# Attention logits from queries and keys in two rounded fp32 parts, two heads in the two halves of TensorE's rows

## The chip, the cores and the metric

The kernel runs on one core of one Trainium2 chip. The metric is the device time of one execution in microseconds (us). The times before are 1162.42, 1163.57 and 1163.80 us, median 1163.57. The profile is one execution of its own, of 1163.27 us.

## The reference

One input x (2048 rows of 640) goes through a gated mix of two branches.

```python
g = sigmoid((x * gate_w).sum(-1))
# A: 32 heads of 20, four segments of 512 rows, causal softmax inside a segment
logits = einsum("bhqd,bhkd->bhqk", qs, ks) * 20 ** -0.5 + mask
a_dot = softmax(logits) @ vs
a_mem = (phi(qs) @ M) / (phi(qs) @ z + 1e-6)     # M, z: sums over the segments before
o = sigmoid(beta) * a_mem + (1 - sigmoid(beta)) * a_dot
a = o @ wo
# B: SwiGLU with an inner size of 1728
b = (silu(x @ w1) * (x @ w3)) @ w2
out = g * a + (1 - g) * b
```

All inputs and outputs are fp32.

## The kernel before

**Dense work.** Weights and activations are split in two parts that TensorE takes at one pass each (`split`: a rounded fp32 copy by ScalarE, the rest by GpSimd or VectorE), and a product is three matmuls (`PASSES`: high x high, high x low, low x high). `proj` runs 15 matmuls of 128 x 512 for a block of 128 features and 512 rows of x; it serves the projections q and k and the gates g and u of the SwiGLU. Down projection (f), values (v) and output projection (op) run matmuls of 320 columns.

**Logits.** A block of q or k (128 features, 512 rows) leaves PSUM in three bf16 parts (`parts`). Six products of parts are kept. The parts are stored to DRAM as six copies for each feature (`qd`, `kd`, one triple, one pair and one single store), so that a head's 20 features are 120 rows. `load_pair` brings two heads' rows into `qst` and `kst` (four buffers each, in turn), by two DMAs on SyncE's queue. For each head there are two rounds of logits:

- `s_unit`: queries as weights, keys streaming, 120 rows, for the four query blocks of 128, of 128, 256, 384 and 512 columns (causal). VectorE takes the row maxima.
- `max_parts` and `max_rows`: the maxima in three bf16 parts are turned and sent by ScalarE's DMA queue into rows 120 to 122 of `qst`; the same rows of `kst` are -1.
- `st_unit`: keys as weights, queries streaming, 123 rows, so that the maximum is subtracted by the matmul; 512, 384, and 128 with 256 columns. ScalarE takes the exponential into P, GpSimd masks the diagonal blocks.

`pv_quad` multiplies P with the values for four heads at once, each in 32 columns of the array (o, 32 matmuls in plain fp32, two passes for each of the 16 calls).

**Order.** The order of TensorE's instructions is written out by the program; the other engines' order is made by a scheduler, except where `here` (keep in program order) pins it. `attention()` is a generator of small steps, ten to a head: t of the third head before, s of this head in three units, now and then an o block. The main loop takes one step of it and then as much dense work as the pacing gives (`credit`, from the dense work of the segment over its slots). `tick()` counts down delayed actions (`after(n, ...)`), `stores()` delayed stores, `w_step()` loads and splits the coming weights. Before attention starts there is a head of projections for the first two segments, and behind it a tail of down and output projection.

Of the kernel before, what the change touches and what calls it, by code (L numbers as in the profile page):

```python
# [27 lines left out]
KR = 6 * DH  # L28
LAG_T, LAG_P, NP, AGE = 3, 4, 4, 4
# [7 lines left out]
def gated_mix(ctx: ExitStack, tc: tile.TileContext, xT, wqk, wv, w13, w2, w2h, wo, beta, out):  # L37
# [7 lines left out]
    qd = [dp.tile([D, 6, L], BF, name=f"qd{c}") for c in range(NSEG)]  # L45
    kd = [dp.tile([D, 6, L], BF, name=f"kd{c}") for c in range(NSEG)]
# [7 lines left out]
    qst = [cp.tile([P, 2, L], BF, name=f"qst{i}") for i in range(NST)]  # L54
    kst = [cp.tile([P, 2, L], BF, name=f"kst{i}") for i in range(NST)]
# [6 lines left out]
    nsT = [cp.tile([P, 32], BF, name=f"ns{i}") for i in range(2)]  # L62
# [4 lines left out]
    def constants():  # L67
        make_identity(nc, ident)
        nc.gpsimd.memset(mask, 0.0)
        nc.gpsimd.affine_select(mask[:, 384:], mask[:, 384:], pattern=[[-1, P]], base=0,  # L70
                                channel_multiplier=1, compare_op=ALU.is_ge, fill=BIG)
        for i in range(2):
            nc.gpsimd.memset(nsT[i], 0.0)
        for i in range(NST):
            nc.gpsimd.memset(qst[i][96:], 0.0)
            nc.gpsimd.memset(kst[i][96:], -1.0)
# [79 lines left out]
    def w_step():  # L156
# [3 lines left out]
        for r in raws:  # L160
            if clock["step"] - r[3] == (AGE // 2 if "exp" in last else AGE + 2) and r[0] >= 7:
                r[4] = last.get("exp", last["act"])
        if raws and raws[0][0] in EARLY:
            if clock["step"] >= 6 + 2 * raws[0][0]:
                w_split()
        elif raws and raws[0][0] < clock["oldest"] + NW and \
                clock["step"] - raws[0][3] >= (AGE if "exp" in last or raws[0][0] < 7 else AGE + 3):
            w_split()
# [88 lines left out]
    def parts(name, ps, phi=None):  # L257


        s = ht_tile([P, 3, L], BF, name)  # L260
        nc.scalar.copy(s[:, 0], ps)
        if phi is not None:
            e = f_tile("phi_t")
            nc.vector.tensor_scalar(e, ps, 0.0, None, op0=ALU.min)
            nc.scalar.activation(e, e, AF.Exp)
# [4 lines left out]
        last["act"] = nc.scalar.copy(s[:, 1], t)  # L270
        nc.gpsimd.tensor_sub(s[:, 2], t, s[:, 1])
        return s

    def q_block(c, mb, i, alloc, oldest=None):
# [6 lines left out]
        dst = qd[c][mb * P:(mb + 1) * P]  # L281
        store_later(dst[:, 0:3], s[:, 0:1].broadcast_to([P, 3, L]), queue=nc.scalar)
        store_later(dst[:, 3:5], s[:, 1:2].broadcast_to([P, 2, L]), queue=nc.scalar)
        store_later(dst[:, 5], s[:, 2], ("q", c, mb))
# [66 lines left out]
    def k_block(c, mb, i, prev):  # L351
# [12 lines left out]
        dst = kd[c][mb * P:(mb + 1) * P]  # L364
        store_later(dst[:, 0:3], s)
        store_later(dst[:, 3:5], s[:, 0:2])
        store_later(dst[:, 5], s[:, 0], ("k", c, mb))
# [14 lines left out]
    def memory_write(c, mb):  # L382
# [12 lines left out]
        nc.scalar.copy(mt, pm[:, :nh * VE].rearrange("p (h e) -> p h e", e=VE))  # L395
# [104 lines left out]
    oall, heads = {}, {}  # L500

    def load_pair(j):

        c, h = divmod(j, H)
        q, k = qst[j // 2 % NST], kst[j // 2 % NST]
# [15 lines left out]
        for i in range(2):  # L521
            o = VE * (h % 8 + i)
            heads[j + i] = dict(c=c, h=h + i, q=q[:, i], k=k[:, i], pair=q, v=bank["v"][:, :, o:o + 32], m=m)

    def s_unit(j, t):
        u = heads[j]
        q, k, m = u["q"], u["k"], u["m"]
        qbs = ((0, 1), (2,), (3,))[t]
        ps = pp.tile([P, L], F32, tag="s", name=f"s{j}_{t}", bufs=2)
        for qb in qbs:  # L530
            n = P * (qb + 1)
            o = P * qb if qb < 2 else 0
            nc.tensor.matmul(ps[:, o:o + n], q[:KR, qb * P:(qb + 1) * P], k[:KR, :n],  # L533
                             start=qb != 1, stop=qb != 0, skip_group_check=True)
        for qb in qbs:
            n = P * (qb + 1)
            o = P * qb if qb < 2 else 0
            junk = sp.tile([P, L], BF, tag="junk", name="junk", bufs=1)
            a = 4 * (u["h"] % 2) + qb
            nc.vector.tensor_tensor_reduce(out=junk[:, :n], in0=ps[:, o:o + n], in1=mask[:, L - n:],  # L540
                                           scale=1.0, scalar=-3.0e38, op0=ALU.add, op1=ALU.max,
                                           accum_out=m[:, a:a + 1])

    def max_parts(j):

        m = heads[j]["m"]
        r = sp.tile([P, 8], F32, tag="nm", name="nm")
        nt = nsT[j // 2 % 2]
        ns = nt[:, :24].rearrange("p (a b) -> p a b", a=3)
        nc.vector.tensor_copy(ns[:, 0], m)  # L550
        nc.vector.tensor_sub(r, m, ns[:, 0])
        nc.vector.tensor_copy(ns[:, 1], r)
        nc.vector.tensor_sub(ns[:, 2], r, ns[:, 1])
        heads[j]["ns"] = nt

    def max_rows(j):
        mr = sp.tile([32, P], BF, tag="mr", name="mr")
        for g in range(4):
            nc.vector.transpose(mr[:, 32 * g:32 * g + 32], heads[j]["ns"][32 * g:32 * g + 32])
        dst = heads[j]["pair"][KR:KR + 3].rearrange("a h (b n) -> a (h b) n", n=P)  # L560
        after(4, lambda: here(nc.scalar.dma_start(dst, mr[:24])))

    def st_unit(j, t):
        u = heads[j]
        q, k = u["q"], u["k"]
        if t == 0:
            u["P32"] = sp.tile([P, 1280], F32, tag="P32", name=f"P{j}", bufs=NP)
        P32 = u["P32"]
        o, n = ((0, 512), (512, 384), (896, 384))[t]
        ps = pp.tile([P, L], F32, tag="t", name=f"t{j}_{t}", bufs=2)  # L570
        if t < 2:
            nc.tensor.matmul(ps[:, :n], k[:KR + 3, t * P:(t + 1) * P], q[:KR + 3, t * P:], start=True, stop=True)  # L572
            src = ps[:, :n]
        else:
            nc.tensor.matmul(ps[:, :P], k[:KR + 3, 384:], q[:KR + 3, 384:], start=True, stop=False,
                             skip_group_check=True)
            nc.tensor.matmul(ps[:, P:384], k[:KR + 3, 256:384], q[:KR + 3, 256:], start=False, stop=True,  # L577
                             skip_group_check=True)
            src = ps[:, :384]
        last["exp"] = nc.scalar.activation(P32[:, o:o + n], src, AF.Exp, scale=SCALE)  # L580
        if t < 2:
            return
        d0 = P32[:, :1024].rearrange("p (a b) -> p a b", a=2)[:, :, :P]
        d1 = P32[:, 896:1152].rearrange("p (a b) -> p a b", a=2)
        for d in (d0, d1):
            nc.gpsimd.affine_select(d, d, pattern=[[0, 2], [1, P]], base=0, channel_multiplier=-1,  # L586
                                    compare_op=ALU.is_ge, fill=0.0)
# [31 lines left out]
    def o_load(c, b):  # L619
# [3 lines left out]
        f = P * b  # L623
        queue = nc.gpsimd if (c, b) != (NSEG - 1, KB - 1) else nc.sync
        while f < P * (b + 1):
            h, e = divmod(f, DH)
            n = min(DH - e, P * (b + 1) - f) if e else max((P * (b + 1) - f) // DH * DH, min(DH, P * (b + 1) - f))
            dst = oall[c][f - P * b:f - P * b + n, b]
# [4 lines left out]
            f += n  # L633
# [51 lines left out]

    def attention():

        for t in range(-3, NJ + LAG_P):
            js, jt, jp = t, t - LAG_T, t - LAG_P
            order = (("-", 0), ("t", 2), ("s", 0), ("m", 0), ("t", 0), ("s", 1), ("p", 0), ("t", 1), ("s", 2))  # L690
            for kind, i in order:
                if kind == "p" and 0 <= jp < NJ and jp % 4 == 3:
                    pv_quad(jp - 3)
                elif kind == "t":
                    h = jt - 1 if i == 2 else jt
                    if 0 <= h < NJ:
                        st_unit(h, i)
                    if i == 2 and t % 2 and t + 3 < NJ:
                        load_pair(t + 3)
                elif kind == "s" and 0 <= js < NJ:  # L700
                    s_unit(js, i)
                    if i == 2 and js % 2:
                        max_parts(js)
                        max_rows(js)
                tick()
                yield t
            tick()
            yield t
# [123 lines left out]
    segs.append((H + LAG_P + 1, seg))  # L832
# [17 lines left out]
    segs.append((2 * H + LAG_P, seg))  # L850
# [4 lines left out]
    segs.append((3 * H + LAG_P + 1, seg))  # L855
# [5 lines left out]
    segs.append((NJ + LAG_P, seg))  # L861
# [4 lines left out]
    for n, (_, g) in enumerate(head):  # L866
# [3 lines left out]
        if n == 0:  # L870
            constants()
        elif n == 9:
            gates()
    stores(True)
    selection()
    att = attention()
    pos = -3
    def begin():

        end, seg = segs.pop(0)  # L880
        n = (end - pos) * 10 - slots % 10
# [86 lines left out]
```

## Time and profile before

| | |
|---|---|
| time of the profiled execution | 1163.27 us |
| its span, first to last instruction | 1161.6 us |
| TensorE busy | 1142.8 us (98%) |
| TensorE weight loads | 872.6 us (75%) |
| VectorE busy | 674.8 us (58%) |
| ScalarE busy | 487.3 us (42%) |
| GpSimd busy | 499.6 us (43%) |
| s, 512 matmuls / t, 256 + 128 + 128 matmuls | lines L533 / L572, L575, L577 |
| o, 1024 matmuls | line L597 |

PE is TensorE's matmul side, PEld its weight loads, DVE VectorE, ACT ScalarE, POOL GpSimd, SP SyncE. A matmul's recorded length holds its latency through the array, and matmuls overlap; the distance between starts in the timeline is what one costs. A row of the timeline has start, length, engine, line, operation, out<-in, shapes and count. A row of the groups has line, engine, operation, out<-in, shapes and count, then busy us, mean ns of one, and the idle time of the engine before them with what ended it.

### The profile page before, as it was taken

How to read it: one execution, taken by the hardware profiler on the slowest of the kernel's cores; microseconds unless marked ns; L12 is line 12 of the kernel's file. 1: busy time of each engine (PE TensorE's matmuls, PEld its weight loads, DVE VectorE, ACT ScalarE, POOL GpSimd, SP SyncE). 2: the span in 40 equal slices, each digit the busy share in tenths (PEclk: the TensorE clock that was granted, in tenths of full speed). 3: DMA queues.
4: the chain of work that ended last, by engine and by line, in shares of the span. 5: the costliest groups of instructions: out<-in, count | busy, mean ns of one | idle time of the engine just before them, and what ended most of it. 6: DMA issues, size and time to landing. Idle time of an engine off the chain costs nothing.

```text
span 1161.6 us, 19926 instructions
## 1 busy us (share of the span) xinstructions
PE 1142.8 (98%) x6953; PEld 872.6 (75%) x6953; DVE 674.8 (58%) x2115; ACT 487.3 (42%) x924; POOL 499.6 (43%) x648
## 2 busy tenths in 40 slices
PE   9999999999999999999999999999999999999998
PEld 7978776767767787878876666768668786876888
DVE  6043585466656654674355888776555776663444
ACT  6255344544343334254365643445543344344140
POOL 7065543244353235264176643353553335355150
PEclk9999999999999999999999999999999999999999
DMA  9266732333433225325377774353542324342122
GB/s 317 91 229 205 236 116 82 100 90 88 106 106 102 64 83 152 90 77 173 125 246 227 250 227 150 104 158 94 161 129 82 91 67 136 93 127 63 47 57 91
DMA packets 108419, 151.89 MB, mean 131 GB/s; under 512 B 14786, under 2 KB 72130, under 8 KB 108318
## 3 DMA queue, kind: packets, MB, share of 16 engines
q1 hardware_dynamic: 80302, 111.66, 32.1%
q10 hardware_dynamic: 22080, 27.40, 6.6%
q0 software_dynamic: 5936, 11.56, 3.3%
q8 instruction: 54, 0.88, 0.3%
q14 instruction: 47, 0.39, 0.1%
HBM read 95.25 MB, written 54.53 MB: 129 GB/s over the span
## 4 chain that ended last, share of the span: by engine, by line
PE 88%; DVE 6%; DMA 2%; issue 2%; ACT 1%; POOL 0%; SPq 0%; POOLq 0%; ACTq 0%; DVEq 0%
PE f L488 16%; PE g L235 16%; PE u L235 15%; PE o L597 6%; PE v L335 6%; PE s L533 6%; PE q L235 5%; PE k L235 5%; PE op L738 4%; PE t L572 4%; DVE junk L540 1%; PE pm L391 1%; PE nd L301 1%; PE t L577 1%; DMA qst<-mr 1%
## 5 line engine op out<-in xcount | busy, mean ns | idle before, releaser
L540 DVE CUSTOM_DVE_ANT_0 junk<-s,mask 128x128 bf16<-128x128 f32 (+3 forms) x512 | 249.1, 487 | 199.0 <-PE s L533 189.9
L580 ACT ACTIVATE P<-t 128x384 f32<-128x384 f32 (+1 forms) x384 | 201.3, 527 | 326.6 <-PE t L572 104.0
L114 POOL TENSOR_TENSOR W<-wr,W 128x640 fp32r<-128x640 f32 (+1 forms) x126 | 196.8, 1567 | 218.6 <-ACT W L113 212.0
L586 POOL TENSOR_SCALAR_AFFINE_SELECT P<-P 128x256 f32<-128x256 f32 x256 | 105.7, 416 | 324.9 <-ACT P L580 320.8
L235 PE MATMUL g<-X,W 128*128 128x512 f32 x840 | 242.0, 423 | 1.2 <-DVE nd_r L308 0.9
L235 PE MATMUL u<-X,W 128*128 128x512 f32 x780 | 225.9, 425 | 0.6 <-DVE nd_r L306 0.6
L488 PE MATMUL f<-W,ht 128*128 128x320 f32 x1312 | 223.4, 321 | 1.5 <-DVE ft L463 1.1
L488 PEld LDWEIGHTS f<-W,ht 128*128 128x128 f32 x1312 | 199.5, 189 | 9.3 <-issue 2.0
L235 PEld LDWEIGHTS g<-X,W 128*128 128x128 f32 x840 | 152.2, 190 | 29.1 <-issue 2.7
L235 PEld LDWEIGHTS u<-X,W 128*128 128x128 f32 x780 | 142.2, 190 | 25.9 <-issue 1.3
L113 ACT CAST W<-wr 128x640 fp32r<-128x640 f32 (+1 forms) x133 | 95.2, 726 | 104.9 <-PE f L488 26.1
L533 PE MATMUL s<-kst,qst 120*128 120x128 bf16 (+3 forms) x512 | 135.2, 305 | 1.8 <-DVE m L540 1.7
L493 DVE SCALAR_TENSOR_TENSOR acc<-f,cgate,acc 128x320 f32<-128x320 f32 x128 | 69.8, 549 | 62.2 <-PE f L488 61.5
L572 PE MATMUL t<-qst,kst 123*128 123x512 bf16 (+1 forms) x256 | 93.1, 364 | 3.1 <-DMA qst<-mr 3.1
L114 POOL TENSOR_TENSOR ht<-ft,ht 128x512 fp32r<-128x512 f32 x52 | 67.0, 1288 | 45.3 <-ACT ht L113 45.1
L533 PEld LDWEIGHTS <-qst 120*128 120x128 bf16 x512 | 44.9, 99 | 51.6 <-issue 42.3
L738 PE MATMUL op<-W,oT 128*128 128x320 f32 x480 | 83.1, 325 | 0.0
L235 PE MATMUL q<-X,W 128*128 128x512 f32 x300 | 81.7, 419 | 0.8 <-DVE X L114 0.4
L235 PE MATMUL k<-X,W 128*128 128x512 f32 x300 | 80.2, 411 | 1.2 <-ACT mt L395 1.2
L335 PE MATMUL v<-W,X 128*128 128x320 f32 (+1 forms) x480 | 75.7, 316 | 0.0
L597 PE MATMUL o<-P,vg 128*32 128x512 f32 (+3 forms) x1024 | 75.6, 436 | 0.0
L738 PEld LDWEIGHTS op<-W,oT 128*128 128x128 f32 x480 | 73.9, 190 | 1.6 <-issue 0.4
(114 smaller groups left out, 1253.9 us busy)
## 6 DMA issues: line engine op xcount, KB each, us to landing
wr<-in_w_dram SPq DMA_DIRECT2D x80, 320.0 KB
qst<-qd SPq DMA_DIRECT2D x64, 240.0 KB
kst<-kd SPq DMA_DIRECT2D x64, 240.0 KB
od<-oq ACTq DMA_DIRECT2D x32, 256.0 KB
qd<-qs ACTq DMA_DIRECT2D x20, 384.0 KB
kd<-ks SPq DMA_DIRECT2D x20, 384.0 KB
wr<-in_wqk_dram SPq DMA_DIRECT2D x21, 320.0 KB
wr<-in_wo_dram SPq DMA_DIRECT2D x20, 320.0 KB
```

Source lines behind the costliest of these rows:

```text
L113: pin(nc.scalar.copy(dst[:, 0], src))
L114: (lo or nc.gpsimd.tensor_sub)(dst[:, 1], src, dst[:, 0].bitcast(F32))
L235: nc.tensor.matmul(ps, w[:, a, kb * P:(kb + 1) * P], x[:, b, kb, :], start=n == 0, stop=n == 14)
L335: nc.tensor.matmul(ps[:, :n1 - n0], x[:, a, kb, lb * P:(lb + 1) * P], wvt[kb][:, b, n0:n1], start=n == 0, stop=n == 14)
L488: nc.tensor.matmul(ps[:, :320], a, b, start=n == 0, stop=n == len(ms) - 1)
L533: nc.tensor.matmul(ps[:, o:o + n], q[:KR, qb * P:(qb + 1) * P], k[:KR, :n], start=qb != 1, stop=qb != 0, skip_group_check=True)
L540: nc.vector.tensor_tensor_reduce(out=junk[:, :n], in0=ps[:, o:o + n], in1=mask[:, L - n:], scale=1.0, scalar=-3.0e38, op0=ALU.add, op1=ALU ...
L572: nc.tensor.matmul(ps[:, :n], k[:KR + 3, t * P:(t + 1) * P], q[:KR + 3, t * P:], start=True, stop=True)
L580: last["exp"] = nc.scalar.activation(P32[:, o:o + n], src, AF.Exp, scale=SCALE)
L586: nc.gpsimd.affine_select(d, d, pattern=[[0, 2], [1, P]], base=0, channel_multiplier=-1, compare_op=ALU.is_ge, fill=0.0)
L597: nc.tensor.matmul(ps[32 * i:32 * i + 32, kb * P:], u["v"][:, kb], u["P32"][:, o:o + n], start=kb == 0, stop=kb == 3, skip_group_check=True)
L738: nc.tensor.matmul(ps[:, :320], oT[0][:, qb % 2, a, kb * P:(kb + 1) * P], ws[kb][:, b, 320 * hf:320 * hf + 320], start=n == 0, stop=n == 14)
```

## The change

- `parts` makes two rounded fp32 parts in place of three bf16 parts; three products are kept, 60 rows a head.
- One DRAM tensor `qkd` for each segment holds, for each head, 66 rows of q and of k side by side: 60 rows of parts, two of padding, four for the maxima. `store_parts` writes it by heads; `pads` writes the padding once (0 for q, -1 for k).
- `load_pair` takes a pair by one DMA of 126 rows on GpSimd's queue (fp32 in DRAM, rounded fp32 in SBUF). The first head lies in rows 0 to 59, its maxima and the second's in rows 62 to 65, and the second head up to row 125. `s_unit` uses rows 0 to 59 and 64 to 125, `t_unit` rows 0 to 63 and 64 to 125.
- s and t of a pair go through both heads in turn, in two PSUM banks; the narrowest matmuls are 256 columns wide. `attention()` has 20 steps a pair, with three places (steps 3, 10, 16) at which s of this pair and t of the pair two before stand together.
- The maxima are two parts, and go by GpSimd's DMA queue.
- In the head, ages of weights (`AGE`) and the place of `selection()` change, and more ScalarE instructions mark `last["act"]`.

```diff
-    qd = [dp.tile([D, 6, L], BF, name=f"qd{c}") for c in range(NSEG)]
-    kd = [dp.tile([D, 6, L], BF, name=f"kd{c}") for c in range(NSEG)]
+    qkd = [dp.tile([H, RH, 2, L], F32, name=f"qkd{c}") for c in range(NSEG)]
...
-    qst = [cp.tile([P, 2, L], BF, name=f"qst{i}") for i in range(NST)]
-    kst = [cp.tile([P, 2, L], BF, name=f"kst{i}") for i in range(NST)]
+    qk = [cp.tile([P, 2, L], FR, name=f"qk{i}") for i in range(NST)]
...
+    def pads():
+
+        pad = cp.tile([P, KB, L], F32, tag="oall", name="pad", bufs=1)
+        here(nc.gpsimd.memset(pad[:16, 0], 0.0))
+        nc.gpsimd.memset(pad[:16, 1], -1.0)
+        for c in range(NSEG):
+            dst = qkd[c].rearrange("(p two) r s n -> p two r s n", two=2)[:, 0, 3 * DH:]
+            here(nc.gpsimd.dma_start(dst, pad[:16, 0:2].rearrange("p (o s) n -> p o s n", o=1)
+                                     .broadcast_to([16, 6, 2, L])))
...
-        s = ht_tile([P, 3, L], BF, name)
-        nc.scalar.copy(s[:, 0], ps)
+        s = ht_tile([P, 2, L], FR, name)
+        last["act"] = nc.scalar.copy(s[:, 0], ps)
...
-        t = f_tile(f"{name}_t")
-        nc.vector.tensor_sub(t, ps, s[:, 0])
+        nc.vector.tensor_sub(s[:, 1], ps, s[:, 0].bitcast(F32))
...
-        last["act"] = nc.scalar.copy(s[:, 1], t)
-        nc.gpsimd.tensor_sub(s[:, 2], t, s[:, 1])
...
+    def store_parts(w, c, mb, s):
+
+        hi, lo = (1, 0) if w == 0 else (0, 2)
+        for h, e, n, r in rows(mb):
+            if n > DH:
+                dst = qkd[c][h:h + n // DH, :3 * DH, w].rearrange("h (d a) n -> h d a n", a=3)
+                for a in (hi, hi + 1):
+                    store_later(dst[:, :, a], s[r:r + n, 0].bitcast(F32))
+                dst = dst[:, :, lo]
+            else:
+                dst = qkd[c][h, 3 * e:3 * (e + n), w].rearrange("(d a) n -> d a n", a=3)
+                store_later(dst[:, hi:hi + 2], s[r:r + n, 0:1].bitcast(F32).broadcast_to([n, 2, L]))
+                dst = dst[:, lo]
+            store_later(dst, s[r:r + n, 1].bitcast(F32), ("qk"[w], c, mb) if r + n == P else None, nc.scalar)
...
-        for t, src in ((q, qd[c]), (k, kd[c])):
-            i = nc.sync.dma_start(t[:KR], src[DH * h:DH * h + 2 * DH].rearrange("(h d) a n -> (d a) h n", h=2))
-            if j < 8:
-                here(i)
+        n = 2 * RH - 6
+        here(nc.gpsimd.dma_start(t[:n], qkd[c].rearrange("h r s n -> (h r) s n")[RH * h:RH * h + n]))
...
+    HALF = ((0, 64), (64, 126))
+
+    def s_unit(p, t):
+
+        u = pairs[p]
+        m = u["m"]
+        ps = [pp.tile([P, L], F32, tag="s", name=f"s{p}_{t}_{i}", bufs=2) for i in range(2)]
+        for qb in ((0, 1), (2,), (3,))[t]:
+            n = max(P * (qb + 1), 256)
+            o = 256 if qb == 1 else 0
+            for i, (r0, r1) in enumerate(((0, 3 * DH), HALF[1])):
+                q, k = u["t"][r0:r1, 0], u["t"][r0:r1, 1]
+                nc.tensor.matmul(ps[i][:, o:o + n], q[:, qb * P:(qb + 1) * P], k[:, :n],
+                                 start=qb != 1, stop=qb != 0, skip_group_check=True)
...
+    def max_rows(p):
...
+        dst = pairs[p]["t"][3 * DH + 2:RH, 0].rearrange("p (b n) -> p b n", n=P)
+        after(5, lambda: here(nc.gpsimd.dma_start(dst, mr[:16])))
...
+    def t_unit(p, t):
...
+        ps = [pp.tile([P, L], F32, tag="t", name=f"t{p}_{t}_{i}", bufs=2) for i in range(2)]
+        for kb, q0, o in (((0, 0, 0),), ((1, P, 0),), ((3, 256, 0), (2, 256, 256)))[t]:
+            for i, (r0, r1) in enumerate(HALF):
+                q, k = u["t"][r0:r1, 0], u["t"][r0:r1, 1]
+                nc.tensor.matmul(ps[i][:, o:o + L - q0], k[:, kb * P:(kb + 1) * P], q[:, q0:],
+                                 start=kb != 2, stop=kb != 3, skip_group_check=True)
...
+    NPAIR = NJ // 2
+    EVENTS = {3: 0, 10: 1, 16: 2}
+
     def attention():
...
+        for t in range(-2, NPAIR + 3):
+            for n in range(20):
+                if t == -2 and n < 16:
+                    continue
+                if n in EVENTS:
+                    if 0 <= t < NPAIR:
+                        s_unit(t, EVENTS[n])
+                        if n == 16:
+                            max_rows(t)
+                    if 0 <= t - 2 < NPAIR:
+                        t_unit(t - 2, EVENTS[n])
+                elif n == 4 and 0 <= t - 3 < NPAIR and t % 2 == 0:
+                    pv_quad(2 * (t - 4))
+                elif n == 19 and 0 <= t + 2 < NPAIR:
+                    load_pair(t + 2)
                 tick()
                 yield t
```

More of the change, by code (lines that the diff above doesn't have):

```diff
@@ L61, in gated_mix @@
     rR = cp.tile([96, L], BF, name="rR")
-    nsT = [cp.tile([P, 32], BF, name=f"ns{i}") for i in range(2)]
+    nsT = [cp.tile([P, 32], FR, name=f"ns{i}") for i in range(2)]
     gate = cp.tile([P, NSEG, 4], F32, name="gate")
@@ L72, in constants @@
         for i in range(2):
[L73 to L76, printed above, removed]
+            nc.gpsimd.memset(nsT[i].bitcast(F32), 0.0)
+    def pads():
[6 more added lines that the diff above has]
+                                     .broadcast_to([16, 6, 2, L])))
     def gates():
@@ L160, in w_step @@
         for r in raws:
-            if clock["step"] - r[3] == (AGE // 2 if "exp" in last else AGE + 2) and r[0] >= 7:
+            if clock["step"] - r[3] == (AGE // 2 if "exp" in last else 2 * AGE) and r[0] >= 7:
                 r[4] = last.get("exp", last["act"])
@@ L166, in w_step @@
         elif raws and raws[0][0] < clock["oldest"] + NW and \
-                clock["step"] - raws[0][3] >= (AGE if "exp" in last or raws[0][0] < 7 else AGE + 3):
+                clock["step"] - raws[0][3] >= (AGE if "exp" in last or raws[0][0] < 7 else 2 * AGE + 1):
             w_split()
@@ L264, in parts, with rows @@
             nc.vector.tensor_scalar(e, ps, 0.0, None, op0=ALU.min)
-            nc.scalar.activation(e, e, AF.Exp)
-        t = f_tile(f"{name}_t")
-        nc.vector.tensor_sub(t, ps, s[:, 0])
+            last["act"] = nc.scalar.activation(e, e, AF.Exp)
+        nc.vector.tensor_sub(s[:, 1], ps, s[:, 0].bitcast(F32))
         if phi is not None:
             nc.vector.scalar_tensor_tensor(phi, ps, 0.0, e, op0=ALU.max, op1=ALU.add)
-        last["act"] = nc.scalar.copy(s[:, 1], t)
-        nc.gpsimd.tensor_sub(s[:, 2], t, s[:, 1])
-        return s
+        return s
+    def rows(b):
+        f = P * b
+        while f < P * (b + 1):
+            h, e = divmod(f, DH)
+            rest = P * (b + 1) - f
+            n = min(DH - e, rest) if e else max(rest // DH * DH, min(DH, rest))
+            yield h, e, n, f - P * b
+            f += n
+    def store_parts(w, c, mb, s):
[11 more added lines that the diff above has]
+            store_later(dst, s[r:r + n, 1].bitcast(F32), ("qk"[w], c, mb) if r + n == P else None, nc.scalar)
     def q_block(c, mb, i, alloc, oldest=None):
@@ L280, in q_block @@
         s = parts(f"qs{c}_{mb}", ps, big["q", c][:, mb * L:(mb + 1) * L] if c else None)
[L281 to L284, printed above, removed]
+        store_parts(0, c, mb, s)
         yield 699
@@ L497, in ffn_down, with load_pair @@
                     nc.sync.dma_start(out[0, c * L + lb * P:c * L + lb * P + P, :], accs[c][:, lb])
-    oall, heads = {}, {}
-    def load_pair(j):
+    oall, heads, pairs = {}, {}, {}
+    def load_pair(p):
+        j = 2 * p
         c, h = divmod(j, H)
-        q, k = qst[j // 2 % NST], kst[j // 2 % NST]
+        t = qk[p % NST]
         for mb in {DH * h // P, (DH * h + 2 * DH - 1) // P}:
@@ L522, in load_pair @@
             o = VE * (h % 8 + i)
[L523 to L542, printed above, removed]
@@ L563, in st_unit @@
-    def st_unit(j, t):
-        u = heads[j]
-        q, k = u["q"], u["k"]
-        if t == 0:
[L567 to L580, printed above, removed]
+            heads[j + i] = dict(c=c, h=h + i, v=bank["v"][:, :, o:o + 32])
@@ new lines, in load_pair @@
+        pairs[p] = dict(t=t, m=m)
+    HALF = ((0, 64), (64, 126))
[10 more added lines that the diff above has]
+                                 start=qb != 1, stop=qb != 0, skip_group_check=True)
+        for i in range(2):
+            for qb in ((0, 1), (2,), (3,))[t]:
+                n = P * (qb + 1)
+                o = 256 if qb == 1 else 0
+                junk = sp.tile([P, L], BF, tag="junk", name="junk", bufs=1)
+                a = 4 * i + qb
+                nc.vector.tensor_tensor_reduce(out=junk[:, :n], in0=ps[i][:, o:o + n], in1=mask[:, L - n:],
+                                               scale=1.0, scalar=-3.0e38, op0=ALU.add, op1=ALU.max,
+                                               accum_out=m[:, a:a + 1])
@@ new lines, in t_unit @@
+    def t_unit(p, t):
+        u = pairs[p]
+        hd = [heads[2 * p + i] for i in range(2)]
+        if t == 0:
+            for i in range(2):
+                hd[i]["P32"] = sp.tile([P, 1280], F32, tag="P32", name=f"P{2 * p + i}", bufs=NP)
+        ps = [pp.tile([P, L], F32, tag="t", name=f"t{p}_{t}_{i}", bufs=2) for i in range(2)]
[4 more added lines that the diff above has]
+                                 start=kb != 2, stop=kb != 3, skip_group_check=True)
+        o, b, n = ((0, 0, 512), (512, 0, 384), (896, P, 384))[t]
+        for i in range(2):
+            P32 = hd[i]["P32"]
+            last["exp"] = nc.scalar.activation(P32[:, o:o + n], ps[i][:, b:b + n], AF.Exp, scale=SCALE)
@@ L581, in st_unit @@
         if t < 2:
             return
[L583 to L587, printed above, removed]
+        for i in range(2):
+            P32 = hd[i]["P32"]
+            d0 = P32[:, :1024].rearrange("p (a b) -> p a b", a=2)[:, :, :P]
+            d1 = P32[:, 896:1152].rearrange("p (a b) -> p a b", a=2)
+            for d in (d0, d1):
+                nc.gpsimd.affine_select(d, d, pattern=[[0, 2], [1, P]], base=0, channel_multiplier=-1,
+                                        compare_op=ALU.is_ge, fill=0.0)
@@ L622, in o_load @@
             oall[c] = cp.tile([P, KB, L], F32, tag="oall", name=f"oall{c}", bufs=1)
-        f = P * b
         queue = nc.gpsimd if (c, b) != (NSEG - 1, KB - 1) else nc.sync
[L625 to L628, printed above, removed]
+        for h, e, n, r in rows(b):
+            dst = oall[c][r:r + n, b]
             if n > DH:
@@ L871, in gated_mix @@
             constants()
+        elif n == 4:
+            pads()
+            selection()
         elif n == 9:
@@ L874, in gated_mix @@
     stores(True)
-    selection()
     att = attention()
-    pos = -3
+    lead = 24
     def begin():
         end, seg = segs.pop(0)
-        n = (end - pos) * 10 - slots % 10
+        n = end * 10 + lead - slots
         return [end, (d for _, g in seg for d in g), sum(c for c, _ in seg) * 1e3 / n]
@@ L893, in gated_mix @@
     while run:
-        if slots == (run[0] + 3) * 10:
+        if slots == run[0] * 10 + lead:
             while step(run) is not None:
@@ L901, in gated_mix @@
         slots += 1
-        pos = slots // 10 - 3
         credit += run[2]
```

62 lines of the change are left out of this document (16 added, 46 removed).

## The prediction

> **What bounds the kernel now.** I read the page first (share of each engine, then the chain that ended last), then PE's waits, and then two stretches of PE's timeline for the durations, since a matmul's recorded length holds its latency and is no price.
>
> ```profile
> span 1161.6 us, 19926 instructions
> PE 1142.8 (98%) x6953; PEld 872.6 (75%) x6953; DVE 674.8 (58%) x2115; ACT 487.3 (42%) x924; POOL 499.6 (43%) x648
> ...
> PEclk9999999999999999999999999999999999999999
> ...
> PE 88%; DVE 6%; DMA 2%; issue 2%; ACT 1%; POOL 0%; SPq 0%; POOLq 0%; ACTq 0%; DVEq 0%
> ```
>
> PE is busy in 98% of the span at the full granted clock, no other engine is above 58%, and the chain runs 88% through PE. So the time is the sum of what PE streams, and a part of the change is worth what it takes from or adds to that stream. PE's own waits are small; the largest two, both of the attention, are
>
> ```profile
> PE t L572 <- DMA qst<-mr: 3.1, 3, 1.7
> PE s L533 <- DVE m L540: 1.7, 4, 0.6
> ```
>
> (us in total, times, longest). Now the price of the logits. In this stretch of PE's timeline (start, length, engine, line, what, shapes, count) dense matmuls of 512 columns surround single logits matmuls; only starts are used.
>
> ```profile
> 500.13 0.39 PE L533 MATMUL s<-kst,qst 120*128 120x512 bf16 x1
> 500.17 1.75 PE L235 MATMUL u<-X,W 128*128 128x512 f32 x6
> 501.75 1.55 PE L235 MATMUL g<-X,W 128*128 128x512 f32 x6
> 503.14 0.23 PE L575 MATMUL t<-qst,kst 123*128 123x128 bf16 x1
> 503.21 0.27 PE L577 MATMUL t<-qst,kst 123*128 123x256 bf16 x1
> 503.24 1.64 PE L235 MATMUL g<-X,W 128*128 128x512 f32 x6
> 504.72 0.34 PE L533 MATMUL s<-kst,qst 120*128 120x128 bf16 x2
> 504.82 2.34 PE L235 MATMUL g<-X,W 128*128 128x512 f32 x9
> 507.00 0.39 PE L572 MATMUL t<-qst,kst 123*128 123x512 bf16 x1
> 507.04 1.05 PE L235 MATMUL g<-X,W 128*128 128x512 f32 x3
> 507.93 0.34 PE L533 MATMUL s<-kst,qst 120*128 120x384 bf16 x1
> 507.97 1.69 PE L235 MATMUL g<-X,W 128*128 128x512 f32 x6
> 509.50 0.86 PE L235 MATMUL u<-X,W 128*128 128x512 f32 x3
> 510.20 0.34 PE L572 MATMUL t<-qst,kst 123*128 123x384 bf16 x1
> 510.24 1.00 PE L235 MATMUL u<-X,W 128*128 128x512 f32 x3
> 511.09 0.39 PE L533 MATMUL s<-kst,qst 120*128 120x512 bf16 x1
> ```
>
> Six g take 503.14 - 501.75 = 1.39, so a rounded fp32 matmul of 512 columns streams in 0.232 us. What is left of each interval is the logits: s of 512, 501.75 - 500.13 - 1.39 = 0.23; t of 128 and 256 together, 504.72 - 503.14 - 1.39 = 0.19; s of 128 and 256, 507.00 - 504.72 - 2.09 = 0.19; t of 512, 0.93 - 0.70 = 0.23; s of 384, 1.57 - 1.39 = 0.18; t of 384, 0.89 - 0.70 = 0.19. A head pays 0.60 for s and 0.61 for t, and nothing for going in and out: the bf16 weights come while the matmul before streams. So the logits are 1.21 x 128 heads = 155 us of PE.
>
> **The streams after.** Keys and queries in two rounded fp32 parts need 60 to 62 rows a head instead of 120 to 123, so that two heads lie in rows 0 to 63 and 64 to 125, and each matmul of one head is followed by the same one of the other. Matmuls under 256 columns are widened to 256 (s of 128, t of 128): 1408 columns a head for s and 1408 for t, against 1280 each. If the two halves run at once, a pair pays 4 matmuls of 256, 2 of 384 and 2 of 512. Rounded fp32 runs at 0.232 for 512 columns (above), and at 320 columns nine f take 1.33 us (below), 0.148 each; the line through both gives 0.119 for 256 and 0.176 for 384. A pair: 4 x 0.119 + 2 x 0.176 + 2 x 0.232 = 1.29, and 64 pairs 83 us. The lower bound is the rate of the o block below, 0.43 for 1024 passed columns: 2816 x 0.42 ns = 1.18, or 76 us. That alone would save 72 to 79 us.
>
> **Going in and out of the halves.** No row of this trace has a matmul in half of the rows. The nearest is the o block, which works in four quarters of the columns:
>
> ```profile
> 484.39 0.34 PE L533 MATMUL s<-kst,qst 120*128 120x384 bf16 x1
> 484.66 2.36 PE L597 MATMUL o<-P,vg 128*32 128x512 f32 x32
> 486.95 1.59 PE L488 MATMUL f<-W,ht 128*128 128x320 f32 x9
> 488.39 0.34 PE L572 MATMUL t<-qst,kst 123*128 123x384 bf16 x1
> 488.43 1.62 PE L488 MATMUL f<-W,ht 128*128 128x320 f32 x9
> 489.90 0.39 PE L533 MATMUL s<-kst,qst 120*128 120x512 bf16 x1
> ...
> 484.66 0.16 PEld L597 LDWEIGHTS o<-P,vg 128*32 128x32 f32 x8 [0.17 <-issue]
> 485.12 0.13 PEld L597 LDWEIGHTS o<-P,vg 128*32 128x32 f32 x4 [0.30 <-issue]
> 485.55 0.13 PEld L597 LDWEIGHTS o<-P,vg 128*32 128x32 f32 x4 [0.30 <-issue]
> ```
>
> Four quarters do run at once: 32 matmuls in 2.29 us. But the way in and out is paid. After the s of 384 (0.18) the o starts only at 0.27: 0.09 in which the array runs empty. Its first group takes 485.12 - 484.66 = 0.46 where the next takes 0.43: 0.03 for weights of 32 columns, which could not be loaded ahead. At the end the nine f behind o take 488.39 - 486.95 = 1.44, where the nine behind the t of 384 take 1.51 - 0.18 = 1.33: 0.11 for fp32 weights of 128 columns. The emptying on the way out is not separately visible; the block itself is 0.12 longer than its streams (0.46 + 0.43 + 4 passes at 3/4 and 1/2 of that + 2 at 1/4 = 2.17), and I take 0.09 again.
>
> [...]
>
> Halves of rows load fp32 weights of 128 columns, so one side costs 0.09 + 0.11 = 0.20 and a visit 0.40. In the changed program's order of PE instructions s and t of a visit stand together: 198 visits (three for each of 64 pairs and six more at the ends, where only s or only t is left), 185 left into dense work and 13 straight into an o block, whose own way in is paid already. That is 198 x 0.20 + 185 x 0.20 = 77 us. Bounds: nothing, if halves of rows are no change at all; 0.18 a visit (35 us), if the weights come while the array empties; 0.62 (about 120 us), if the two halves' weights come one after the other. I take 77, as the o rows show both the emptying and the load. All 32 o blocks now go out into fp32 work (7 went into bf16 t before): 0.7 us.
>
> Sum on PE: 83 + 77 + 1 - 155 = +6.
>
> **What else moves.** The exponents' shift rows go from ACT's queue to POOL's, in two parts, and the next pair's q and k in one load on POOL's queue, instead of two on SP's. One pair lasts
>
> ```profile
> L533 PE MATMUL s<-kst,qst x512: 216/300/394, 131.0 to 1056.1; 120*128 120x128 bf16 x43, 120*128 120x512 bf16 x43, 120*128 120x384 bf16 x43, 120*128 120x256 bf16 x42
> ...
> L630 POOL DMA_DIRECT2D oall<-od x19: 633/656/820, 285.8 to 1061.2; - x19
> ...
> DMA to landing us min/median/max: 4.2/4.7/6.6
> ...
> oall<-od POOLq DMA_DIRECT2D x11, 240.0 KB, 4.5
> ...
> L271 POOL TENSOR_TENSOR qs<-qs_t,qs 128x512 bf16<-128x512 f32 x20 | 24.1, 1206 | 9.6 <-ACT qs L270 9.0 <-POOL sel L96 0.3
> L271 POOL TENSOR_TENSOR ks<-ks_t,ks 128x512 bf16<-128x512 f32 x20 | 23.3, 1165 | 10.5 <-ACT ks L270 8.4 <-PE s L533 2.1
> ```
>
> 925 us / 64 = 14.5 us, 0.72 for each of the 20 slots. The load is given out in slot 19 and read in slot 3 of the second pair on: 24 slots, 17 us, against 4.2 to 6.6 us for a POOL load of 240 KB; this one is 504 KB and rounds on the way, so up to 10 us is an estimate by twice the median, and still hidden. The shift rows have 23 slots, more than before, so the 3.1 us of waits for them should go. POOL gains 128 issues x 0.66 = 84 us at most and loses the third part's subtraction, 24.1 + 23.3 = 47 us: 499.6 becomes about 537, 46%, with no path to PE. Queued behind the two DMAs on POOL are the weights' low parts (L114) and the masks of P (L586); the issue waits for the t of the pair four before, which stands three slots earlier on PE, so I cost it at nothing; if that cover is gone, see the third rival. ACT loses the third part's rounding, DVE two of four small operations a pair; neither bounds. More, smaller stores (split by heads) leave on SP and ACT; they have the same 17 us, and the bytes are the same (three copies of 256 KB a block for six of 128 KB). All six logits matmuls of a visit wait for two banks of s and two of t that DVE and ACT must have read; visits stand six slots, 4 us, apart. DVE's reductions come in bursts of up to four, so dense banks are freed later now and then: I allow +1. At the head and the tail PE's work is unchanged.
>
> Sum: 6 - 3 + 1 = +4 on the profiled 1163.3 (span 1161.6 and 1.7 around it), which is 0.3 below the median of the runs. So 1167.5. Own bounds of this case: streams at 76 give 7 less, the emptying at 0.12 instead of 0.09 gives 11 more: 1160 to 1179.
>
> **Rivals.** (1) The way in and out is cheaper (the other side: faster). If halves of rows share the array with full matmuls, or the weights come while the array empties, 35 us or less replaces 77: 1167.5 - 42 = 1125.5, and with no price at all 1090. It is faster as soon as a visit costs under about 0.38. For it: bf16 visits cost nothing now. Against it: those keep all 128 rows in use, and the o block pays on both sides. (2) The halves don't run side by side. If the two halves' weights come one after the other, each pair of matmuls lasts at least 0.21 (two loads of 0.11): a pair 6 x 0.21 + 2 x 0.23 = 1.72 instead of 1.29, 28 us, and each visit's first load 0.11 more, 22 us: 1217. If the matmuls themselves take turns, 83 us more: 1250, the case in which the change doesn't do what it says; each tenth of the overlap that is lost costs 8 us, so a loss of three tenths gives 1192. Against all three: o's first eight loads end within 0.16 us, and its four quarters pass 1024 columns each in 0.43, no slower than one dense stream (2 x 0.232).
>
> [...]
>
> (3) POOL's queue is late: its order is fixed, and a load of 504 KB that waits behind a mask of P or a weight's part arrives after slot 3. It decides from 17 us between its slot and its landing; each us beyond that, for 64 pairs, is 64 us; a quarter of the pairs late by 1 us gives 1184. For it: POOL waits long for ACT and is in order; against: 10 us of slack.
>
> **The numbers.** Forecast 0.56, rival 1 0.24, rival 2 0.13 (0.05 a partial loss of the overlap, 0.05 loads in turn, 0.03 matmuls in turn), rival 3 0.07. About 0.2% (2.3 us) is what a measurement of this kernel can tell from no change. Within the forecast's own range I give 0.08 to faster, 0.12 to the same and 0.36 to slower; with the rivals faster is 0.32, the same 0.12, slower 0.56. The range takes in rival 1 down to its 35 us (half of its chance lies below) and rival 2 up to a loss of between four and five tenths of the overlap: 1124 to 1205.
>
> **What would show it.** In the timeline: pairs of s and t starting within 0.01 us; the first matmul of a visit 0.20 late, and the dense one behind it 0.20 late; a visit of 256, 256 and 512 about 0.87 us, of 384 and 384 about 0.75. PE stays at 98%, s and t waiting for no DMA. Wrong: a dense matmul at its usual 0.23 behind the last t (rival 1), starts of the two heads 0.1 or more apart (rival 2), or PE waiting for qk (rival 3).

## The result and the profile after

The changed kernel takes 1251.74 us (1245.31 to 1252.81) against 1163.68 before: ratio 1.0744, 95% interval 1.0705 to 1.0783. It is 88 us slower; 1167.5 was forecast, with a range up to 1205. That the time is close to rival 2's 1250 is chance: the two halves do run side by side, as the timeline shows below.

The page after (same parts as before):

```profile
span 1250.2 us, 19931 instructions
PE 1181.2 (94%) x6953; PEld 916.4 (73%) x6953; DVE 657.0 (53%) x1987; ACT 455.3 (36%) x884; POOL 521.3 (42%) x734
...
PEclk9899799999999999999999889999999999999999
...
PE 70%; DMA 19%; issue 3%; DVE 3%; POOL 1%; ACT 1%; SPq 1%; ACTq 0%; POOLq 0%; DVEq 0%
PE g L241 16%; PE f L510 16%; PE u L241 15%; DMA qkd<-qs 7%; DMA qkd<-ks 7%; PE s L559 5%; PE o L619 5%; PE op L756 4%; PE v L360 4%; PE t L595 3%; DMA wr<-in_wqk_dram 2%; PE nd L326 1%; POOL W L120 1%; DMA vg<-vd 1%; PE k L241 1%
```

PE is no longer nearly the whole chain (70% in place of 88%): a fifth of it is DMA, most of it the stores of the parts (qkd<-qs, qkd<-ks), 14% of the span. PE's granted clock falls below nine tenths in four slices, all in the stretches in which PE idles; before, it never did. The o blocks are landmarks that both kernels have; these are the first, the ninth, the seventeenth and the last of the 32, as the chain in order of time shows them (start, length), before and then after:

```profile
174.25 2.29 PE o L597 x32
...
394.33 2.29 PE o L597 x32
...
703.01 2.29 PE o L597 x32
...
1076.58 2.29 PE o L597 x32
```

```profile
221.44 2.29 PE o L619 x32
...
441.28 2.29 PE o L619 x32
...
791.87 2.29 PE o L619 x32
...
1164.50 2.29 PE o L619 x32
```

Up to the first block 47 us are lost, from the first to the ninth nothing (219.8 after against 220.1 before), from the ninth to the seventeenth 42, from there to the last nothing (372.6 against 373.6). The attention that runs beside gates and down projection costs what it cost before. The loss lies where blocks of q and k are projected and stored: the head, and the second half's projections.

The stretches of the windows view after (length, PE busy, then the other engines; granted clock, DMA share and GB/s last):

```profile
0.00:200.00 200.00, 166.47 (x798) 136.68 (x799) 65.10 (x155) 60.48 (x121) 54.23 (x82) 0.91 0.61 171
200.00:500.00 300.00, 300.00 (x1824) 227.81 (x1823) 169.08 (x550) 119.42 (x227) 141.57 (x195) 1.00 0.38 100
500.00:800.00 300.00, 270.40 (x1555) 208.94 (x1553) 158.96 (x476) 105.72 (x215) 116.09 (x169) 0.95 0.51 151
```

Between 200 and 500 us PE never stops. In the head it idles for 34 of 200 us and runs at 0.91 of its clock in the mean.

The view of the line that issues the stores, before and after (engine, operation, tiles, count: min/median/max ns of one issue, first and last start; then who waited for a landing):

```profile
L253 ACTq DMA_DIRECT2D qd<-qs x40: 366/367/416, 11.7 to 678.9; - x40
L253 SPq DMA_DIRECT2D qd<-qs x20: 319/328/890, 15.7 to 680.1; - x20
...
  ACT cR L83: 3.0, 1
```

```profile
L259 SPq DMA_DIRECT2D qkd<-qs x72: 247/700/5031, 11.7 to 762.2; - x72
L259 ACTq DMA_DIRECT2D qkd<-qs x52: 246/508/4087, 13.0 to 765.2; - x52
...
  ACT qs L267: 34.9, 7
  ACT V L367: 23.4, 4
  ACT mt L417: 21.7, 5
  ACT ks L267: 20.4, 4
  ACT P L600: 16.0, 3
```

Two things are seen. An issue that took 0.37 us, at most 0.42, on ACT takes up to 4.1 there, and up to 5.0 on SP (0.89 before); what a long issue waits for, the trace doesn't say. And ACT's copies (qs and ks at L267, V, mt, P) start late, by waits that the profile puts down to the landing of an earlier store. The chain in the head shows where the wait stands (start, length):

```profile
12.61 9.35 DMA qkd<-qs
...
21.98 0.75 ACTq L259
...
22.77 0.49 ACTq L259
...
23.30 0.59 ACT qs L267
```

A store that SP gave out at 12.61 lands at 21.96. Only then does ACT issue two stores of its own, and the copy of the next block of q comes right behind them. So here it is not the copy that waits, for a free buffer say, but the store in front of it. The semaphores in the traces fit that: the transfers of SP and ACT share eight, in both kernels, and not one of them (572 before, 508 after) was issued before the transfer that had its semaphore last had landed. The store that lands at 21.96 has number 105, and the next transfer with 105 is the one that ACT issues at 21.98. SP's stores wait in the same way (us in total, times, longest):

```profile
SPq L259 <- DMA qkd<-qs: 37.9, 23, 5.4
SPq L259 <- DMA qkd<-ks: 30.8, 20, 4.3
```

That is 69 us, where the kernel before waits 3.0 for stores of q and k. The copies that stand behind ACT's stores come late (in the view of L259, qs, V, mt, ks and P wait 116 us), and PE, which needs their banks of PSUM, stands still:

```profile
PE k L241 <- ACT mt L417: 9.1, 4, 4.4
PE t L595 <- ACT P L600: 9.0, 4, 3.9
...
PE v L360 <- ACT gate L369: 8.4, 1, 8.4
```

And the visits in PE's timeline after, which the prediction priced:

```profile
499.62 2.68 PE L241 MATMUL u<-X,W 128*128 128x512 f32 x11
502.23 0.50 PE L559 MATMUL s<-qk 60*128 60x512 f32 x2
502.56 0.41 PE L595 MATMUL t<-qk 64*128 64x256 f32 x4
502.90 3.75 PE L241 MATMUL g<-X,W 128*128 128x512 f32 x15
506.49 3.60 PE L241 MATMUL u<-X,W 128*128 128x512 f32 x15
```

Both s of 512 columns are one row of 0.50 us, and the first t follows 0.33 behind their start, where two in turn would need 0.46: they overlap. The visit lasts 502.90 - 502.23 = 0.67, its streams are 0.232 + 2 x 0.119 = 0.47, so 0.20 is left, as read here for the first weights (0.10 between s and t) and the emptying of the array; the fifteen g behind take 3.59 in place of 3.48, 0.11 for their first weights. With the 0.05 to 0.09 on the way in that is 0.36 to 0.40 a visit, as priced.

### The profile page after: what moved, and what is told of

It is laid out like the page before. It is cut to its first block, busy times and chain, and to the rows that moved or that the text cites. A ratio compares the mean times of both kernels' runs of the same rounds, so it can differ in the third digit from the quotient of the medians.

```text
span 1250.2 us, 19931 instructions
## 1 busy us (share of the span) xinstructions
PE 1181.2 (94%) x6953; PEld 916.4 (73%) x6953; DVE 657.0 (53%) x1987; ACT 455.3 (36%) x884; POOL 521.3 (42%) x734
## 4 chain that ended last, share of the span: by engine, by line
PE 70%; DMA 19%; issue 3%; DVE 3%; POOL 1%; ACT 1%; SPq 1%; ACTq 0%; POOLq 0%; DVEq 0%
PE g L241 16%; PE f L510 16%; PE u L241 15%; DMA qkd<-qs 7%; DMA qkd<-ks 7%; PE s L559 5%; PE o L619 5%; PE op L756 4%; PE v L360 4%; PE t L595 3%; DMA wr<-in_wqk_dram 2%; PE nd L326 1%; POOL W L120 1%; DMA vg<-vd 1%; PE k L241 1%
## 5 line engine op out<-in xcount | busy, mean ns | idle before, releaser
L600 ACT ACTIVATE P<-t 128x384 f32<-128x384 f32 (+1 forms) x384 | 182.0, 525 | 321.0 <-PE t L595 205.6
L241 PE MATMUL g<-X,W 128*128 128x512 f32 x840 | 222.2, 406 | 0.7 <-DVE nd_r L333 0.7
L510 PE MATMUL f<-W,ht 128*128 128x320 f32 x1312 | 208.5, 314 | 2.1 <-DVE ft L485 1.4
L241 PE MATMUL u<-X,W 128*128 128x512 f32 x780 | 206.4, 405 | 0.3 <-DVE oall L682 0.3
L510 PEld LDWEIGHTS f<-W,ht 128*128 128x128 f32 x1312 | 194.3, 189 | 13.7 <-issue 6.8
L559 PE MATMUL s<-qk 60*128 60x256 f32 (+5 forms) x512 | 94.1, 401 | 5.2 <-DVE m L567 5.2
L559 PEld LDWEIGHTS s<-qk 60*128 60x128 f32 (+1 forms) x512 | 43.6, 184 | 63.5 <-issue 52.0
L360 PEld LDWEIGHTS v<-W,X 128*128 128x128 f32 x480 | 75.5, 200 | 18.0 <-ACT gate L369 8.6
L595 PE MATMUL t<-qk 62*128 62x256 f32 (+5 forms) x512 | 77.7, 330 | 9.1 <-ACT P L600 9.0
L241 PEld LDWEIGHTS q<-X,W 128*128 128x128 f32 x300 | 60.2, 208 | 22.6 <-ACT pkn L400 3.3
```

Source lines behind the costliest of these rows:

```text
L241: nc.tensor.matmul(ps, w[:, a, kb * P:(kb + 1) * P], x[:, b, kb, :], start=n == 0, stop=n == 14)
L360: nc.tensor.matmul(ps[:, :n1 - n0], x[:, a, kb, lb * P:(lb + 1) * P], wvt[kb][:, b, n0:n1], start=n == 0, stop=n == 14)
L510: nc.tensor.matmul(ps[:, :320], a, b, start=n == 0, stop=n == len(ms) - 1)
L559: nc.tensor.matmul(ps[i][:, o:o + n], q[:, qb * P:(qb + 1) * P], k[:, :n], start=qb != 1, stop=qb != 0, skip_group_check=True)
L595: nc.tensor.matmul(ps[i][:, o:o + L - q0], k[:, kb * P:(kb + 1) * P], q[:, q0:], start=kb != 2, stop=kb != 3, skip_group_check=True)
L600: last["exp"] = nc.scalar.activation(P32[:, o:o + n], ps[i][:, b:b + n], AF.Exp, scale=SCALE)
```

## The experiments

The theory after the result, S: the stores by heads are slow to land, and buffers and queues back up to PE. Four versions of it: the shape of a store decides (S1), the number of stores (S2), the stores on ACT's queue (S3), the padding (S4). The rival: the halves of rows, or the loads on POOL's queue.

**flat_pool: no gaps in DRAM, whole-block stores.** Heads move to rows 0 and 64 of the tile, and each one's maxima lie behind its 60 rows.

```diff
-    qkd = [dp.tile([H, RH, 2, L], F32, name=f"qkd{c}") for c in range(NSEG)]
+    qkd = [dp.tile([D, 3, 2, L], F32, name=f"qkd{c}") for c in range(NSEG)]
...
+        dst = qkd[c][P * mb:P * mb + P, :, w]
+        store_later(dst[:, hi:hi + 2], s[:, 0:1].bitcast(F32).broadcast_to([P, 2, L]))
+        store_later(dst[:, lo], s[:, 1].bitcast(F32), ("qk"[w], c, mb), nc.scalar)
...
+        for i in range(2):
+            r = 3 * DH * (h + i)
+            here(nc.gpsimd.dma_start(t[64 * i:64 * i + 3 * DH],
+                                      qkd[c].rearrange("f a s n -> (f a) s n")[r:r + 3 * DH]))
```

> DRAM holds the parts by features (640 x 3 copies x q and k) without gaps between heads, so that each copy of a block leaves in one store of 128 rows (two stores a block in place of seven to nine), there is no padding to write, and a pair is loaded by two transfers of 60 rows on GpSimd's queue, the maxima by two small ones. TensorE's instructions are those of the change. If the loss sits in the stores by heads (theory S), the head and the second stretch of q and k lose their 46 and 39 us: 1163 to 1170 us. If it sits in the two halves of rows on TensorE or in loads on GpSimd's queue (rival), the time stays at 1240 to 1260, or grows with twice as many GpSimd transfers.

Measured: 1167.31 us, ratio 1.0045 (1.0028 to 1.0062) to before. The whole loss but 4.7 us is gone, with TensorE's visits unchanged and twice as many GpSimd transfers. Both rivals fall. (The change has five or seven stores a block, 248 in 40 blocks, and not seven to nine; the kernel before has three.) The chain is PE's again:

```profile
PE 91%; DVE 3%; issue 2%; DMA 2%; POOL 1%; ACT 0%; SPq 0%; POOLq 0%; ACTq 0%; DVEq 0%
```

**flat_sliced: the same layout, stored in the change's pieces.**

```diff
+        for h, e, n, r in rows(mb):
+            dst = qkd[c][P * mb + r:P * mb + r + n, :, w]
+            if n > DH:
+                for a in (hi, hi + 1):
+                    store_later(dst[:, a], s[r:r + n, 0].bitcast(F32))
...
```

> As flat_pool, but each block still leaves in the pieces of the change (by heads, the high part twice), only into a layout without gaps, so that a piece of 120 or 100 rows is one run of rows instead of 6 or 5 heads of 20. If what counts is over how many DMA engines one store spreads (S1), most of the loss goes: 1165 to 1185 us. If it is the number of stores that SyncE and ScalarE must issue (S2), little goes: 1220 to 1250, less what the padding cost.

Measured: 1172.28 us, ratio 1.0085 (1.0061 to 1.0108). Cutting the blocks into pieces costs about 5 us (1172.3 - 1167.3), not 80: S2 falls.

**lo_sp: the low parts' stores on SP's queue.** `store_later(..., nc.scalar)` loses its last argument in the changed kernel.

> The change with the low parts' stores on SyncE's queue instead of ScalarE's, nothing else. If the loss comes from ScalarE standing still while its queue can't issue a store (S3), 40 us or more go: 1200 or less. If the stores themselves are slow and the buffers of the parts come free late (S1), the time stays within 1235 to 1265, as all stores now stand in one queue.

Measured: 1243.64 us, 8 us less than the change by the medians and 5 by the ratios to before. S3 falls as the whole of the loss. The run doesn't price ACT's standing still: ACT's other stores, of V and of o, still wait until a part's store on SP has landed, so that the view of line L259 there has V waiting 23.8 us and P 14.2.

**pads_late: padding of three segments after the head.** `pads(range(1))` in the head, `pads(range(1, NSEG))` behind it.

> The change with the padding of three of the four segments written after the head instead of in it. If the four padding stores, 15 us to landing each, hold up the stores in the head (S4), up to 25 us go from the head: 1225 to 1235. If not, 1245 to 1255; the second stretch of q and k, which has no padding, lost 39 us anyway.

Measured: 1254.79 us (1251.38 to 1258.19). S4 falls.

**flat_gap: one unused row behind each head.** This is the run that isolates S1: the stores of flat_sliced, one by one, into rows that are no longer evenly spaced.

```diff
-    qkd = [dp.tile([D, 3, 2, L], F32, name=f"qkd{c}") for c in range(NSEG)]
+    qkd = [dp.tile([H, 3 * DH + 1, 2, L], F32, name=f"qkd{c}") for c in range(NSEG)]
...
+                dst = qkd[c][h:h + n // DH, :3 * DH, w].rearrange("h (d a) n -> h d a n", a=3)
```

> flat_sliced with one unused row behind each head's 60 rows in DRAM, and nothing else: the number of stores, their bytes, the padding and the loads are those of flat_sliced, only the large pieces are 6 or 5 heads of 20 rows again in place of one run of 120 or 100. [...] If the padding or the larger load were the cause, it stays at 1170 to 1180.

Measured: 1246.19 us, ratio 1.0715 (1.0695 to 1.0735). One row of gap costs 74 us. By the shapes in the trace the large pieces are 6 x 20 x 512 and 5 x 20 x 512 here, and 120 x 512 and 100 x 512 in flat_sliced. The same line's view, flat_sliced and then flat_gap:

```profile
L251 SPq DMA_DIRECT2D qkd<-qs x72: 252/340/818, 13.7 to 682.1; - x72
L251 ACTq DMA_DIRECT2D qkd<-qs x52: 246/333/1430, 14.5 to 683.0; - x52
...
  ACT qs L259: 9.7, 3
```

```profile
L251 SPq DMA_DIRECT2D qkd<-qs x72: 247/707/2919, 11.5 to 758.3; - x72
L251 ACTq DMA_DIRECT2D qkd<-qs x52: 246/692/2369, 12.9 to 759.0; - x52
...
  ACT qs L259: 46.7, 8
```

The same 72 and 52 issues take twice as long in the median, ACT's qs copies wait 46.7 us behind stores instead of 9.7, and SP's stores wait 68 us for earlier ones to land instead of 17.5 (none in flat_pool). So the gap is the cause, and what it changes in a store is the shape of the large pieces. The packets of SP's queue (q1) and ACT's (q10) differ with it, of flat_gap and then of flat_sliced (packets, MB, share of the 16 engines):

```profile
q1 hardware_dynamic: 47470, 82.82, 21.9%
...
q10 hardware_dynamic: 12896, 24.39, 6.0%
```

```profile
q1 hardware_dynamic: 48062, 82.82, 23.5%
...
q10 hardware_dynamic: 13192, 24.39, 6.0%
```

With the same bytes flat_sliced has 592 packets more on SP and 296 more on ACT, all of them small (under 512 bytes the pages count 23834 against 22946). They go with the large pieces, 80 on SP and 40 on ACT (the small ones are 64 on each): 592 / 80 = 296 / 40 = 7.4 for each. So the gap also changes how the large pieces are cut into packets. Over how many DMA engines a store spreads, no view shows; that this is what makes them slow was the author's estimate and is not shown. The gap also moves the rows' addresses. The loads of the same rows land as soon as before (3.8 us in the median against 3.9); that stores to such addresses are slower by themselves was not tested.

**flat_apart: s and t in visits of their own.**

```diff
+    LATER = {6: 0, 13: 1, 18: 2}
...
+                elif n in LATER and 0 <= t - 2 < NPAIR:
+                    t_unit(t - 2, LATER[n])
```

> flat_pool with s and t of a pair in visits of their own (t three, three and two steps later), so that TensorE goes 375 times from dense work into the halves of rows instead of 198. At 0.40 us a visit, as the prediction priced it, 177 more visits cost 71 us: 1235 to 1240. If a visit costs little (rival 1), 1170 to 1200.

Measured: 1232.96 us, a little under what was expected. 65.7 us for 177 visits: 0.37 each, against the 0.40 of the prediction. Rival 1 falls.

**flat_near: the o block right behind its visit.** `pv_quad` is called in step 3 behind `t_unit` instead of in step 4.

> flat_pool with the o block right behind the visit of its step, without dense work between: 31 of 32 blocks instead of 13. Saves 18 ways out at 0.20 us and changes the way in at nothing: 3.6 us less than flat_pool, 1163 to 1164.5. If a way from the halves of rows to the quarters of columns costs as much as one over dense work, 1167.

Measured: 1162.68 us, ratio 1.0002 (0.9992 to 1.0013): 5 us less than flat_pool by the ratios, a little more than the 3.6 of 18 ways out.

**flat_sp_near: loads and maxima on SP's queue.**

> flat_near with the pair's loads and the maxima on SyncE's queue instead of GpSimd's (the bytes in DRAM are rounded already). TensorE's stream is the same, and nothing in flat_pool waits for GpSimd's transfers, so 1162 to 1165, at most 2 us from flat_near.

Measured: 1165.74 us, ratio 1.0018 (1.0009 to 1.0027). GpSimd's queue is not the price: without it the kernel is 1.9 us slower by the ratios and 3.1 by the medians, a little outside what was expected. Why was not tried.

**flat_narrow: no widening to 256 columns.** `n = P * (qb + 1)` in `s_unit`, `(3, 384, P)` for `(3, 256, 0)` in `t_unit`.

> flat_near without the widening to 256 columns: s of the first query block and t of the last key block are 128 columns wide. If rounded fp32 streams 128 columns at the rate of 256 and more, two pairs of matmuls in a pair of heads fall from 0.116 to about 0.06 us: 2 x 0.055 x 64 = 7 us less, 1155 to 1157, faster than the kernel before. If it takes four passes under 256 columns, as the widening suggests, they rise to 0.21 us: 12 us more, 1174 to 1176.

Measured: 1162.78 us, ratio 0.9994 (0.9985 to 1.0003). Neither. The same visit in flat_near and in flat_narrow:

```profile
408.28 0.50 PE L545 MATMUL s<-qk 60*128 60x512 f32 x2
408.62 0.40 PE L587 MATMUL t<-qk 62*128 62x256 f32 x4
408.94 1.43 PE L233 MATMUL u<-X,W 128*128 128x512 f32 x5
```

```profile
407.48 0.50 PE L545 MATMUL s<-qk 60*128 60x512 f32 x2
407.81 0.40 PE L587 MATMUL t<-qk 62*128 62x128 f32 x4
408.14 1.20 PE L233 MATMUL u<-X,W 128*128 128x512 f32 x4
```

0.66 us in both. The reading: the weights of the next pair take 0.11 and hide whatever a shorter stream gains. Only the last stream of a visit has no pair's weights behind it, which the next run uses.

**flat_last: the 128 columns at the end of their visits.**

```diff
-        for qb in ((0, 1), (2,), (3,))[t]:
+        for qb in ((1, 0), (2,), (3,))[t]:
...
-        for kb, q0, o in (((0, 0, 0),), ((1, P, 0),), ((3, 384, P), (2, 256, 256)))[t]:
+        for kb, q0, o in (((0, 0, 0),), ((1, P, 0),), ((2, 256, 256), (3, 384, P)))[t]:
```

> flat_narrow with the matmuls of 128 columns moved to the end of their visits (first visit of a pair: t before s, and s of 256 before s of 128; third: t of 256 before t of 128). In flat_narrow the next pair's weights, 0.11 us, hid the gain of 128 columns; at the end of a visit the weights behind it are paid in any case. If 128 columns stream in 0.053 us and the weights are the floor, 2 x 0.053 x 64 = 7 us less than flat_narrow: 1155 to 1157, below the kernel before. If the short matmuls cost something else, 1162.

Measured: 1154.46 us, ratio 0.9934 (0.9921 to 0.9946): 0.7% faster than the kernel before, 8 us below flat_narrow by the medians and 7 by the ratios, where 7 were expected.

```profile
404.92 0.50 PE L545 MATMUL s<-qk 60*128 60x512 f32 x2
405.25 0.34 PE L587 MATMUL t<-qk 62*128 62x256 f32 x4
405.53 2.37 PE L233 MATMUL u<-X,W 128*128 128x512 f32 x9
```

405.53 - 404.92 = 0.61 in place of 0.66: at the end of a visit 128 columns fewer save 0.05, about what they take at the rate of 0.232 for 512.

## Why the prediction was wrong

- What bounds the kernel: right, for the kernel before. After the change it isn't so in two stretches, and the prediction looked for a new bound on POOL's queue, not on SP's and ACT's.
- Streams and visits (83 + 77 + 1 - 155 = +6, with waits +4): right. flat_pool, which has them without the slow stores (and with two loads a pair and no padding), is 4.7 us slower than before (1167.31 against 1162.56), and a visit measured on its own costs 0.37 us. That halves of rows pay as the o block's quarters do, 0.40 a visit, was the author's estimate from the o rows; the trace before has no matmul in half of the rows.
- The step that failed is one sentence: that more, smaller stores leave on SP and ACT, have the same 17 us, and carry the same bytes. It was costed at nothing. It measured 79 us (1246.19 - 1167.31), of which about 5 for the cutting into pieces and 74 for the shape of the large ones. Two errors are in it. The price of a store was taken from its bytes, although its shape had changed, from one run of 128 rows to 6 heads of 20. And its cover was taken from the wrong reader: the loads come 17 us later, but the next stores come sooner. In the head a block of q follows each 3.5 us (15 matmuls of 0.232), with five or seven stores in place of three, and no store was issued while the transfer that had its semaphore last was under way (9.35 us in the chain above). Behind such a store on ACT stand ACT's copies (116 us of waits in the whole run), and behind them stands PE. The prediction named what is queued behind the new transfers on POOL and left out SP's and ACT's queues. What flat_gap leaves of the change's loss, about 5 us (1251.74 - 1246.19), no run divides; the padding and the one load a pair are among what differs.
- Rival 1 (visits cheap): refuted by flat_apart. Rival 2 (no overlap, 1250): refuted by the timeline and by flat_pool, although the time fits. Rival 3 (POOL's queue late): in the changed kernel PE waits for no load of q and k, which lands in 4.9 us in the median, and moving the loads and maxima off POOL's queue gains nothing. None of the rivals was the store path.
- The waits for maxima that should go did go: no wait of PE for them is among those of flat_pool or of the changed kernel.

## What to carry to other kernels

When a change alters the layout of a transfer, price the transfer anew by its shape: one unused row between heads turned runs of 120 rows into 6 heads of 20 and cost 74 us with the same bytes and the same number of stores. Ask of a store not only when its data is read, but what waits to be issued until it has landed, and which engine's work stands behind that. Before believing a total that fits a rival, look in the timeline for that rival's signature.

## What the runs showed of the hardware

- Rounded fp32 matmuls in the two halves of the rows start together (the two s of 512 columns in the visit above 3 ns apart) and overlap fully (both s of 512 columns are over 0.33 us behind their start, 0.10 of it for the weights); going from full rows to halves and back costs 0.37 us (65.7 us for 177 visits), nearly the 0.40 that the o block's quarters suggested.
- Inside a visit, fp32 weights of 128 columns (0.11 us) were a floor for each pair of matmuls, as these runs are read: 128 instead of 256 columns gained nothing in front of another pair (0.66 us both), and 0.05 us at the end of the visit.
- With large stores of 6 x 20 and 5 x 20 rows in place of runs of 120 and 100, SP's issues of q's stores took 0.71 us in the median instead of 0.34, with the same bytes.
- Where PE idled, its granted clock fell too: 0.91 in the first 200 us and 0.95 between 500 and 800, against 1.00 between 200 and 500. The loss in these stretches holds both; in flat_pool, where PE hardly idles there, the clock is 1.00 in all three.
